# Conditioning vector on the GpSimd queue, attention output by channel instead of by token with crossbar transposes

## Chip, core and metric

The kernel runs on one core of a Trainium2 chip. The metric is the device time of one execution in microseconds, the median of several runs. The engines named below are TensorE (PE, with its weight loads as PEld), VectorE (DVE), ScalarE (ACT), GpSimd (POOL) and SyncE (SP). SP here only issues DMAs and waits.

## What is computed

The attention half of a diffusion transformer block with adaptive layer norm. B = 2 batches, N = 256 tokens, D = 1152 channels, all arrays bf16:

```
mod = (silu(c) @ w_mod).reshape(B, 6, 1, D)
shift_a, scale_a, gate_a = mod[:, 0], mod[:, 1], mod[:, 2]      # the other three are not used
h = layernorm(x) * (1 + scale_a) + shift_a
q, k, v = split(h @ wqkv)
p = softmax(q @ k.T * D ** -0.5)
out = x + gate_a * (p @ v @ wo)
```

## The kernel before

The 512 tokens are four tiles of 128 (tiles 0 and 1 are batch 0, tiles 2 and 3 batch 1), and the 1152 channels are nine blocks of 128. Every operation goes through `op` (line 35), which records the engine, what is read and what is written. `emit` (line 72) turns this into one stream per engine with semaphore waits. So each engine, and each queue of DMAs, runs in the order in which the operations are recorded. A DMA queue is the instruction stream of the engine that issues it: the loads of x tile 2, 0 and 1 and all weights stand in SP's, those of `c` (line 295) and of x tile 3 (line 297) in ACT's. POOL begins with the identity matrices and small constants (lines 322 to 329).

**Start.** `ORDER` (line 169) writes out by hand how the engines' first work is interleaved. PE turns `c` (`cT`, line 506), then x tile 2, runs four matmuls on zeros (`warm`), then turns the other x tiles. ACT sums x tile by tile (`sum_x`, line 386) and then makes silu(c) with DVE and POOL, which ends in `scT_sb`: for each block of channels 32 columns, of which the first two are the two batches' values and the others zero. DVE centres and scales the turned x. The scale groups of w_mod (`s_mm`, line 441) and the key weights arrive in pieces, and keys are accumulated block by block into seven banks of PSUM. Queries, values and scores follow.

**From the scores on** (lines 738 to 817). `v_last` computes the last 128 channels of v turned, and a crossbar DMA turns them back. `v_tile(i)` computes the first 1024 channels of v for one token tile, in two pieces of 512. `score` and `softmax` leave the probabilities in `e_sb`, and `p_T` has SP turn them by a crossbar DMA into `pT_sb`. The gate row is `silu(c) @ w_mod[gate]`: 36 matmuls (line 752) put it into a bank in four quarters of 288 channels, each in a strip of 32 partitions. `scr_sb`, a copy of `scT_sb` made by POOL (line 739), repeats each batch's value 16 times, so that each strip has 16 equal rows per batch. Eight DMAs (line 764) copy them to all 128 partitions of `gate_rep`, each of the 16 rows 8 times.

`pv(i)` (line 671) is attention output for one token tile: the stationary operand is `pT_sb` (128 keys by 128 tokens), the moving one `v_sb` in pieces of 384 channels, two matmuls per piece. Three pieces are evacuated by ACT and DVE in turn, and a crossbar DMA on SP turns the tile into `pvT_sb` (channels on partitions), which the output projection reads. `pv(0)` and `pv(1)` come after the first piece of v tile 2, `pv(2)` and `pv(3)` after the projection of tile 0.

**Output projection** (lines 782 to 817). For each token tile, columns in pieces of 384: nine matmuls into one bank (line 792), the gate multiplied by DVE (line 805), x added (line 808), and a store by SP. After each piece of tile 1 DVE multiplies three blocks of `wo` with the gate (`fold`, line 773); tile 3's last columns use these and have the residual added in one step (line 797). Banks are taken in a ring of eight (`next_bank`, line 647).

Of the kernel before, what the change touches and what calls it, by code (L numbers as in the profile page):

```python
# [6 lines left out]
ALU = mybir.AluOpType  # L7
# [3 lines left out]
PE = mybir.EngineType.PE  # L11
DVE = mybir.EngineType.DVE
AC = mybir.EngineType.Activation
POOL = mybir.EngineType.Pool
SP = mybir.EngineType.SP
# [6 lines left out]
class _Prog:  # L22
# [12 lines left out]
    def op(self, eng, fn, r=(), w=(), dma=False, extra=()):  # L35
        o = _Op()
        o.eng, o.fn, o.dma = eng, fn, dma
        o.sem = o.val = None
        o.inc = False
        deps = set(extra)  # L40
        for k in r:
            if k[0] == "ps":
                continue
            p = self.last_w.get(k)
            if p is not None and not (p.eng == eng == PE):
                deps.add(p)
            self.readers.setdefault(k, []).append(o)
        for k in w:
            if k[0] == "ps":
                continue  # L50
            for q in self.readers.get(k, ()):
                if q is not o and (q.dma or dma or q.eng != eng):
                    deps.add(q)
            p = self.last_w.get(k)
            if p is not None and p is not o and not (p.eng == eng == PE):
                deps.add(p)
            self.readers[k] = [o] if k in r else []
            self.last_w[k] = o
        for k in set(r) | set(w):
            if k[0] != "ps":  # L60
                continue
            accesses = self.bank.setdefault(k, {})
            for e, q in accesses.items():
                if e != eng:
                    deps.add(q)
            accesses[eng] = o
        deps.discard(o)
        o.deps = deps
        self.ops.append(o)
        return o  # L70
# [71 lines left out]
B = 2  # L142
NTOK = 256
D = 1152
T = B * NTOK
P = 128
DC = D // P
# [11 lines left out]
GW = 288  # L159
# [37 lines left out]
def _build(nc, es, x, c, wqkv, wo, w_mod, out):  # L197
    bf16 = dt.bfloat16
# [12 lines left out]
    xnT_sb = sb("xnT_sb", [P, DC, T], bf16)  # L211
    hT_sb = sb("hT_sb", [P, DC, T], bf16)
    qkT_sb = sb("qkT_sb", [P, 2 * DC, T], bf16)
    v_sb = sb("v_sb", [P, TT, D], bf16)
# [22 lines left out]
    d1_sb = sb("d1_sb", [P, DC, 2], f32)  # L237
    rc_sb = sb("rc_sb", [P, DC, 2], f32)
    scT_sb = sb("scT_sb", [P, DC, 32], bf16)
    scr_sb = sb("scr_sb", [P, DC, B, 16], bf16)  # L240
    s1_sb = sb("s1_sb", [P, DC, 2], f32)
    sh_sb = sb("sh_sb", [P, DC, 32], f32)
    gaterow_sb = sb("gaterow_sb", [P, GW], bf16)
# [48 lines left out]
        op(SP, lambda e: e.dma_start(wq_sb[:, k0:k1, c0:c1], wq_v[:, k0:k1, c0:c1]),  # L292
           w=[("w", tag, k) for k in range(k0, k1)], dma=True)

    op(AC, lambda e: e.dma_start(c_sb[:, :], c[:, :]), w=[("c",)], dma=True)
    load_x(SP, 2)
    load_x(AC, 3)
    op(AC, lambda a: a.preload_act_table_set("natural_log_exp_and_others"))
# [38 lines left out]
    def evac(eng, dst, src, r, w):  # L337
        if eng == DVE:
            op(DVE, lambda v: v.tensor_copy(dst, src), r=r, w=w)  # L339
        else:  # L340
            op(AC, lambda a: a.activation(dst, src, ACT.Copy), r=r, w=w)  # L341
# [305 lines left out]
    def next_bank():  # L647
        bnk = ring[rot[0] % 8]
        rot[0] += 1
        return bnk  # L650
# [15 lines left out]
        op(SP, lambda e: e.dma_start(v_sb[:, :, c0:c1], vT_sb[:, :], transpose=True),  # L666
           r=[("vT",)], w=[("v", i, 2) for i in range(TT)], dma=True)

    AP_ = [(0, 384), (384, 768), (768, 1152)]

    def pv(i):
        b = i // 2
        for q, (c0, c1) in enumerate(AP_):
            bank = next_bank()
            for sbk in range(2):
                op(PE, lambda pe, sbk=sbk, c0=c0, c1=c1, bank=bank: pe.matmul(  # L676
                    ps[bank][:, 0:c1 - c0], pT_sb[:, b, sbk, (i % 2) * P:(i % 2 + 1) * P],
                    v_sb[:, 2 * b + sbk, c0:c1], start=(sbk == 0), stop=(sbk == 1)),
                   r=[("v", 2 * b + sbk, n) for n in range(3) if VP[n][0] < c1 and VP[n][1] > c0] + [("pT", b, i % 2)],
                   w=[("ps", bank)])  # L680
            evac(AC if (3 * i + q) % 2 == 0 else DVE, bass.AP(xnT_sb, i * D + c0, [[DC * T, P], [1, c1 - c0]]),
                 ps[bank][:, 0:c1 - c0],
                 [("ps", bank)], [("at", i, q)])
        op(SP, lambda e: e.dma_start(pvT_sb[:, :, i * P:(i + 1) * P], bass.AP(xnT_sb, i * D, [[DC * T, P], [1, D]]), transpose=True),
           r=[("at", i, q) for q in range(3)], w=[("pv", i)] + [("h0", cc, i) for cc in range(DC)], dma=True)

    def v_tile(i, pieces=(0, 1)):
        for q in pieces:
            c0, c1 = VP[q]
            bank = next_bank()  # L690
            for k in range(DC):
                op(PE, lambda pe, k=k, c0=c0, c1=c1, bank=bank: pe.matmul(  # L692
                    ps[bank][:, 0:c1 - c0], hT_sb[:, k, i * P:(i + 1) * P], wq_sb[:, k, 2 * D + c0:2 * D + c1],
                    start=(k == 0), stop=(k == DC - 1)),
                   r=[("w", "v", k), ("hT", k, i // 2)], w=[("ps", bank)])
            nev[0] += 1
            dst, src, sc = v_sb[:, i, c0:c1], ps[bank][:, 0:c1 - c0], rstd_sb[:, i:i + 1]
            rk, wk = [("ps", bank), ("rstd", i)], [("v", i, q)]
            if nev[0] % 2:
                op(AC, lambda a, dst=dst, src=src: a.activation(dst, src, ACT.Copy, scale=sc), r=rk, w=wk)  # L700
            else:
                op(DVE, lambda v, dst=dst, src=src: v.tensor_scalar(dst, src, sc, None, op0=ALU.mult), r=rk, w=wk)  # L702
# [30 lines left out]
    def p_T(i):  # L733
# [1 line left out]
        op(SP, lambda e: e.dma_start(pT_sb[:, b, :, qt * P:(qt + 1) * P], e_sb[:, i, :], transpose=True),  # L735
           r=[("e", i)], w=[("pT", b, qt)], dma=True)

    src = bass.AP(scT_sb, 0, [[DC * 32, P], [32, DC], [1, B], [0, 16]])
    op(POOL, lambda g: g.tensor_scalar(scr_sb[:, :, :, :], src, 1.0, 0.0, op0=ALU.mult, op1=ALU.add),
       r=[("scT",)], w=[("scr",)])  # L740
    v_last()
    v_tile(0)
    sbanks = [score(i) for i in range(TT)]
# [6 lines left out]
    for k in range(DC):  # L750
        for j in range(4):
            op(PE, lambda pe, k=k, j=j, bank=bank: pe.matmul(  # L752
                ps[bank][32 * j:32 * (j + 1), 0:GW], scr_sb[:, k, :, :],
                wgate_ap[:, k, j * GW:(j + 1) * GW], start=(k == 0), stop=(k == DC - 1)),
               r=[("wgate",), ("scr",)], w=[("ps", bank)])
    op(AC, lambda a, bank=bank: a.activation(gaterow_sb[:, :], ps[bank][:, 0:GW], ACT.Copy),
       r=[("ps", bank)], w=[("grow",)])
    v_tile(2, (0,))
    pv(0)
    pv(1)  # L760
    for b in range(B):
        for j in range(4):
            row = bass.AP(gaterow_sb, (32 * j + 16 * b) * GW, [[GW, 16], [0, 8], [1, GW]])
            op(SP, lambda e, b=b, j=j, row=row: e.dma_start(gate_rep[:, b, j * GW:(j + 1) * GW], row),
               r=[("grow",)], w=[("gate", b, j)], dma=True)
    v_tile(2, (1,))
    v_tile(3)


    LC = 768  # L770
# [11 lines left out]
    for i in range(TT):  # L782
        b = i // 2
        cols = [(0, 384), (384, 768), (768, 1152)] if i < TT - 1 else [
            (0, 384), (384, 768), (768, 1024), (1024, 1152)]
        for (c0, c1) in cols:
            n = c1 - c0
            bank = next_bank()
            gated = i == TT - 1 and c0 >= LC
            for k in range(DC):  # L790
                rhs = wog_ap[:, k, c0 - LC:c1 - LC] if gated else wo_ap[:, k, c0:c1]
                op(PE, lambda pe, i=i, k=k, rhs=rhs, n=n, bank=bank: pe.matmul(  # L792
                    ps[bank][:, 0:n], pvT_sb[:, k, i * P:(i + 1) * P], rhs,
                    start=(k == 0), stop=(k == DC - 1)),
                   r=[("pv", i), ("wog", k) if gated else ("wo",)], w=[("ps", bank)])
            if gated:
                op(DVE, lambda v, i=i, c0=c0, c1=c1, n=n, bank=bank: v.tensor_tensor(  # L797
                    xo_sb[:, i, c0:c1], ps[bank][:, 0:n], x_sb[:, i, c0:c1], ALU.add),
                   r=[("ps", bank), ("x", i)], w=[("o", i, c0)])
                store(i, c0, c1)  # L800
                continue
            s = nst[0] % 4
            nst[0] += 1
            gk = [("gate", b, j) for j in range(4) if j * GW < c1 and (j + 1) * GW > c0]
            op(DVE, lambda v, b=b, c0=c0, c1=c1, n=n, bank=bank, s=s: v.tensor_tensor(  # L805
                ga_sb[:, s, 0:n], ps[bank][:, 0:n], gate_rep[:, b, c0:c1], ALU.mult),
               r=[("ps", bank)] + gk, w=[("ga", s)])
            op(DVE, lambda v, i=i, c0=c0, c1=c1, n=n, s=s: v.tensor_tensor(
                xo_sb[:, i, c0:c1], x_sb[:, i, c0:c1], ga_sb[:, s, 0:n], ALU.add),
               r=[("x", i), ("ga", s)], w=[("o", i, c0)])  # L810
            store(i, c0, c1)
            if i == 0 and c1 == D:
                pv(2)
                pv(3)
            if i == 1:
                for k in range(nst[0] % 3 * 3, nst[0] % 3 * 3 + 3):
                    fold(k)
# [34 lines left out]
```

## Time and profile before

| What | Value |
|---|---|
| median of 3 runs | 98.04 us (97.77 to 98.43) |
| profiled execution | 97.77 us, of it 96.0 us from the first to the last instruction |
| granted TensorE clock | 1.000 (mean) |
| chain that ended last | PE 75%, SP's queue 10%, DMA 9% of the span |
| matmuls of L676 (attention output) | 24, 128x384 |
| crossbar transposes of `pvT_sb` | 4, 3.3 us from issue to landing |
| gate row DMAs (L764) | 8 of 72 KB, 2.7 us from issue to landing |
| transposes of `pT_sb` | 4, 2.3 us to landing |

The span counts from the first instruction of the program to the last; the time of the execution lies around it. A row of the chain of waits reads: start in us, length in us, engine, what it writes, line, how many. A row of the timeline adds the operation, its output and input, and in brackets how long the engine had been idle and what ended that. "ACTq" and "SPq" are DMA issues in the queue of ACT and SP; how long a DMA then takes to land stands apart.

### The profile page before, as it was taken

The page shows a single profiled execution, that of the slowest core. Times are in us where ns is not written, and L with a number is a line of the kernel's source. Part 1 is how long each engine was busy: PE and PEld are TensorE (multiplying, and loading weights), DVE is VectorE, ACT ScalarE, POOL GpSimd, SP SyncE. Part 2 cuts the span into 40 slices and gives each one's busy share as a digit, 9 for nine tenths or more (in the row PEclk, how much of TensorE's full clock was granted, in tenths as well). Part 3 has the DMA queues.
Part 4 walks back from the last instruction along what each step waited for, and adds up shares of the span by engine and source line. Part 5 has one row for each costly group of instructions (what it writes and reads, how often), then busy time and mean ns, then how long its engine had stood idle before and what let it go on. Part 6 is the DMA issues. An engine that isn't in the chain of part 4 may idle for free.

```text
span 96.0 us, 1715 instructions
## 1 busy us (share of the span) xinstructions
PE 90.6 (94%) x685; PEld 49.8 (52%) x693; DVE 51.6 (54%) x133; ACT 31.7 (33%) x65; POOL 2.4 (2%) x13
## 2 busy tenths in 40 slices
PE   5998899979999999999999999999999999999990
PEld 1666555444544454444444487455544655665570
DVE  1157984840458649305602075564631567899571
ACT  2778897956541200004120203336402014000000
POOL 5040000000000000000000000000000000000000
PEclk9999999999999999999999999999999999999999
DMA  2999999999999999999999993111296742931222
GB/s 50 332 294 355 328 314 350 352 321 336 363 366 366 381 339 353 387 394 390 393 391 393 391 330 75 38 27 27 46 200 106 123 98 76 206 94 43 91 70 82
DMA packets 25403, 23.21 MB, mean 242 GB/s; under 512 B 7346, under 2 KB 21426, under 8 KB 25396
## 3 DMA queue, kind: packets, MB, share of 16 engines
q1 hardware_dynamic: 25248, 22.81, 78.4%
q10 hardware_dynamic: 148, 0.30, 1.0%
q8 instruction: 5, 0.08, 0.3%
q14 instruction: 2, 0.02, 0.1%
HBM read 19.76 MB, written 1.18 MB: 218 GB/s over the span
## 4 chain that ended last, share of the span: by engine, by line
PE 75%; SPq 10%; DMA 9%; issue 1%; ACT 1%; DVE 0%
PE psbank L492 28%; PE psbank L792 18%; PE psbank L692 16%; DMA wm_sb<-in_w_mod_dram 9%; SPq L292 7%; PE psbank L708 4%; PE psbank L676 4%; PE psbank L660 2%; SPq L285 1%; PE psbank L436 1%; SPq L281 1%; PE psbank L752 1%; ACT qkT_sb L341 1%; PE psbank L415 0%; DVE xo_sb L797 0%
## 5 line engine op out<-in xcount | busy, mean ns | idle before, releaser
L492 PE MATMUL psbank<-pvT_sb,wq_sb 128*128 128x512 bf16 (+1 forms) x82 | 18.0, 366 | 0.7 <-DVE pvT_sb L477 0.3
L492 PE MATMUL psbank<-hT_sb,wq_sb 128*128 128x512 bf16 x79 | 17.5, 379 | 0.2 <-issue 0.2
L792 PE MATMUL psbank<-wm_sb,pvT_sb 128*128 128x384 bf16 x99 | 16.4, 326 | 0.0
L692 PE MATMUL psbank<-wq_sb,hT_sb 128*128 128x512 bf16 x70 | 15.8, 379 | 0.2 <-issue 0.2
L792 PEld LDWEIGHTS psbank<-wm_sb,pvT_sb 128*128 128x128 bf16 x99 | 9.7, 98 | 6.5
L492 PEld LDWEIGHTS psbank<-hT_sb,wq_sb 128*128 128x128 bf16 x81 | 7.9, 98 | 9.4
L492 PEld LDWEIGHTS psbank<-pvT_sb,wq_sb 128*128 128x128 bf16 x86 | 7.9, 98 | 8.3 <-DVE pvT_sb L477 0.6
L341 ACT ACTIVATE qkT_sb<-psbank 128x512 bf16<-128x512 f32 x9 | 5.0, 603 | 19.5 <-PE psbank L492 19.5
L692 PEld LDWEIGHTS psbank<-wq_sb,hT_sb 128*128 128x128 bf16 x72 | 7.0, 98 | 8.2 <-DVE nb_sb L723 0.2
L339 DVE CAST qkT_sb<-psbank 128x512 bf16<-128x512 f32 x9 | 5.7, 684 | 9.2 <-PE psbank L492 9.2
L805 DVE TENSOR_TENSOR ga_sb<-psbank,gate_rep 128x384 bf16<-128x384 f32 x11 | 6.1, 555 | 4.2 <-PE psbank L792 4.2
L485 DVE SCALAR_TENSOR_TENSOR hT_sb<-std_sb,sh_sb,pvT_sb 128x256 bf16<-128x256 f32 x18 | 7.3, 480 | 0.1
L702 DVE TENSOR_SCALAR v_sb<-psbank,rstd_sb 128x512 bf16<-128x512 f32 x4 | 3.0, 750 | 7.7 <-PE psbank L692 7.7
L341 ACT ACTIVATE xnT_sb<-psbank 128x384 bf16<-128x384 f32 (+2 forms) x9 | 4.7, 546 | 6.5 <-PE psbank L676 6.4
L383 DVE TENSOR_TENSOR xnT_sb<-xnT_sb,nm_sb 128x512 bf16<-128x512 bf16 (+1 forms) x9 | 5.6, 656 | 0.0
L700 ACT ACTIVATE v_sb<-psbank,rstd_sb 128x512 bf16<-128x512 f32 x4 | 2.7, 682 | 7.9 <-PE psbank L692 7.9
L399 ACT ACTIVATE junk_sb<-x_sb,nmu_sb 128x1152 bf16<-128x1152 bf16 x4 | 5.0, 1251 | 0.1
L333 PE MATMUL psbank<-warm_sb 128*128 128x512 bf16 x9 | 3.9, 590 | 1.2 <-DVE warm_sb L320 1.2
L388 ACT ACTIVATE junk_sb<-x_sb 128x1152 bf16<-128x1152 bf16 x4 | 4.6, 1159 | 1.0 <-DMA x_sb<-in_x_dram 1.0
L725 ACT ACTIVATE e_sb<-s_sb,nb_sb 128x256 bf16<-128x256 bf16 x4 | 2.0, 508 | 8.2 <-DVE nb_sb L723 8.2
L339 DVE COPY xnT_sb<-psbank 128x512 bf16<-128x512 bf16 (+1 forms) x5 | 2.1, 447 | 4.1 <-PE psbank L349 4.0
L676 PE MATMUL psbank<-v_sb,pT_sb 128*128 128x384 bf16 x24 | 4.2, 326 | 0.0
(73 smaller groups left out, 73.1 us busy)
## 6 DMA issues: line engine op xcount, KB each, us to landing
wq_sb<-in_wqkv_dram SPq DMA_DIRECT2D x3, 864.0 KB, 11.0
wm_sb<-in_w_mod_dram SPq DMA_DIRECT2D x1, 2592.0 KB, 16.1
wm_sb<-in_wo_dram SPq DMA_DIRECT2D x1, 2592.0 KB, 21.8
wq_sb<-in_wqkv_dram SPq DMA_DIRECT2D x4, 448.0 KB, 8.3
wm_sb<-in_w_mod_dram SPq DMA_DIRECT2D x3, 576.0 KB, 7.5
wm_sb<-in_w_mod_dram SPq DMA_DIRECT2D x1, 1440.0 KB, 11.0
wq_sb<-in_wqkv_dram SPq DMA_DIRECT2D x6, 224.0 KB, 6.9
wq_sb<-in_wqkv_dram SPq DMA_DIRECT2D x2, 576.0 KB, 10.1
```

The source lines that it names most:

```text
L292: op(SP, lambda e: e.dma_start(wq_sb[:, k0:k1, c0:c1], wq_v[:, k0:k1, c0:c1]), w=[("w", tag, k) for k in range(k0, k1)], dma=True)
L339: op(DVE, lambda v: v.tensor_copy(dst, src), r=r, w=w)
L341: op(AC, lambda a: a.activation(dst, src, ACT.Copy), r=r, w=w)
L383: op(eng, lambda e: e.tensor_tensor(ap, ap, nm, ALU.add), r=[("xnT", cc, i) for i in tiles] + nk, w=[("xnT", cc, i) for i in tiles])
L388: op(AC, lambda a: a.activation(junk_sb[:, :], x_sb[:, i, :], ACT.Copy, scale=sc, accum_out=dst[:, i:i + 1]), r=[("x", i)], w=[("junk", 0) ...
L399: op(AC, lambda a: a.activation(junk_sb[:, :], x_sb[:, i, :], ACT.Square, bias=nmu_sb[:, i:i + 1], scale=1.0, accum_out=sq_sb[:, i:i + 1]) ...
L485: op(DVE, lambda v: v.scalar_tensor_tensor(hT_sb[:, cc, lo:hi], std_sb[:, lo:hi], sh_sb[:, cc, b:b + 1], h0T_sb[:, cc, lo:hi], op0=ALU.mul ...
L492: op(PE, lambda pe: pe.matmul(ps[bank][:, lo:hi], wq_sb[:, k, col * P:(col + 1) * P], src[:, k, lo:hi], start=(k == 0) if start is None el ...
L676: op(PE, lambda pe, sbk=sbk, c0=c0, c1=c1, bank=bank: pe.matmul(ps[bank][:, 0:c1 - c0], pT_sb[:, b, sbk, (i % 2) * P:(i % 2 + 1) * P], v_s ...
L692: op(PE, lambda pe, k=k, c0=c0, c1=c1, bank=bank: pe.matmul(ps[bank][:, 0:c1 - c0], hT_sb[:, k, i * P:(i + 1) * P], wq_sb[:, k, 2 * D + c0 ...
L792: op(PE, lambda pe, i=i, k=k, rhs=rhs, n=n, bank=bank: pe.matmul(ps[bank][:, 0:n], pvT_sb[:, k, i * P:(i + 1) * P], rhs, start=(k == 0), s ...
L805: op(DVE, lambda v, b=b, c0=c0, c1=c1, n=n, bank=bank, s=s: v.tensor_tensor(ga_sb[:, s, 0:n], ps[bank][:, 0:n], gate_rep[:, b, c0:c1], ALU ...
```

## The change

The conditioning vector's DMA moves from ACT's queue to POOL's, where it stands ahead of the identity and constants. x tile 3 is then the first DMA on ACT's queue.

`pv` becomes a function of a batch and a pair of channel blocks. The stationary operand is now `v_sb` (128 keys by 128 channels), the moving one `pT_sb` of a whole batch (256 tokens), and the result is already turned: two channel blocks share a bank and go by one evacuation straight into `pvT_sb`. There are five pairs per batch, the last with one block. The four crossbar transposes go. All ten calls stand after v tile 3 and before the projection, instead of in two places.

`scr_sb` and its copy go: the gate matmuls read `scT_sb` itself, so each strip has one row per batch, and each gate DMA reads that row 128 times. These DMAs no longer have transposes of `pvT_sb` before them on SP.

```
-    scr_sb = sb("scr_sb", [P, DC, B, 16], bf16)
...
-    op(AC, lambda e: e.dma_start(c_sb[:, :], c[:, :]), w=[("c",)], dma=True)
+    op(POOL, lambda e: e.dma_start(c_sb[:, :], c[:, :]), w=[("c",)], dma=True)
     load_x(SP, 2)
     load_x(AC, 3)
...
-    AP_ = [(0, 384), (384, 768), (768, 1152)]
-    def pv(i):
...
-                    ps[bank][:, 0:c1 - c0], pT_sb[:, b, sbk, (i % 2) * P:(i % 2 + 1) * P],
-                    v_sb[:, 2 * b + sbk, c0:c1], start=(sbk == 0), stop=(sbk == 1)),
...
-        op(SP, lambda e: e.dma_start(pvT_sb[:, :, i * P:(i + 1) * P], bass.AP(xnT_sb, i * D, [[DC * T, P], [1, D]]), transpose=True),
-           r=[("at", i, q) for q in range(3)], w=[("pv", i)] + [("h0", cc, i) for cc in range(DC)], dma=True)
...
-    src = bass.AP(scT_sb, 0, [[DC * 32, P], [32, DC], [1, B], [0, 16]])
-    op(POOL, lambda g: g.tensor_scalar(scr_sb[:, :, :, :], src, 1.0, 0.0, op0=ALU.mult, op1=ALU.add),
-       r=[("scT",)], w=[("scr",)])
...
-                ps[bank][32 * j:32 * (j + 1), 0:GW], scr_sb[:, k, :, :],
+                ps[bank][32 * j:32 * (j + 1), 0:GW], scT_sb[:, k, :],
...
-    v_tile(2, (0,))
-    pv(0)
-    pv(1)
     for b in range(B):
         for j in range(4):
-            row = bass.AP(gaterow_sb, (32 * j + 16 * b) * GW, [[GW, 16], [0, 8], [1, GW]])
+            row = bass.AP(gaterow_sb, (32 * j + b) * GW, [[GW, 1], [0, P], [1, GW]])
...
-    v_tile(2, (1,))
+    v_tile(2)
     v_tile(3)
+    def pv(b, pair):
+        ccs = [cc for cc in (2 * pair, 2 * pair + 1) if cc < DC]
+        bank = next_bank()
+        for h, cc in enumerate(ccs):
+            for sbk in range(2):
+                op(PE, lambda pe, h=h, cc=cc, sbk=sbk: pe.matmul(
+                    ps[bank][:, h * NTOK:(h + 1) * NTOK],
+                    v_sb[:, 2 * b + sbk, cc * P:(cc + 1) * P], pT_sb[:, b, sbk, :],
+                    start=(sbk == 0), stop=(sbk == 1)),
+                   r=[("v", 2 * b + sbk, cc // 4), ("pT", b, 0), ("pT", b, 1)], w=[("ps", bank)])
+        n = len(ccs)
+        evac(AC if pair % 2 == 0 else DVE,
+             pvT_sb[:, ccs[0]:ccs[0] + n, b * NTOK:(b + 1) * NTOK],
+             ps[bank][:, 0:n * NTOK].rearrange("p (c t) -> p c t", c=n),
+             [("ps", bank)], [("pv", cc, b) for cc in ccs] + [("h0", cc, 2 * b + n) for cc in ccs for n in (0, 1)])
+    for b in range(B):
+        for pair in range(5):
+            pv(b, pair)
...
-                   r=[("pv", i), ("wog", k) if gated else ("wo",)], w=[("ps", bank)])
+                   r=[("pv", k, b), ("wog", k) if gated else ("wo",)], w=[("ps", bank)])
...
-            if i == 0 and c1 == D:
-                pv(2)
-                pv(3)
```

More of the change, by code (lines that the diff above doesn't have):

```diff
@@ L667, in v_last, with v_tile @@
            r=[("vT",)], w=[("v", i, 2) for i in range(TT)], dma=True)
-    AP_ = [(0, 384), (384, 768), (768, 1152)]
-    def pv(i):
[L672 to L676, printed above, removed]
-                    ps[bank][:, 0:c1 - c0], pT_sb[:, b, sbk, (i % 2) * P:(i % 2 + 1) * P],
-                    v_sb[:, 2 * b + sbk, c0:c1], start=(sbk == 0), stop=(sbk == 1)),
[L679 to L683, printed above, removed]
-        op(SP, lambda e: e.dma_start(pvT_sb[:, :, i * P:(i + 1) * P], bass.AP(xnT_sb, i * D, [[DC * T, P], [1, D]]), transpose=True),
-           r=[("at", i, q) for q in range(3)], w=[("pv", i)] + [("h0", cc, i) for cc in range(DC)], dma=True)
-    def v_tile(i, pieces=(0, 1)):
-        for q in pieces:
-            c0, c1 = VP[q]
+    def v_tile(i):
+        for q, (c0, c1) in enumerate(VP[:2]):
             bank = next_bank()
@@ L752, in _build @@
             op(PE, lambda pe, k=k, j=j, bank=bank: pe.matmul(
-                ps[bank][32 * j:32 * (j + 1), 0:GW], scr_sb[:, k, :, :],
+                ps[bank][32 * j:32 * (j + 1), 0:GW], scT_sb[:, k, :],
                 wgate_ap[:, k, j * GW:(j + 1) * GW], start=(k == 0), stop=(k == DC - 1)),
-               r=[("wgate",), ("scr",)], w=[("ps", bank)])
+               r=[("wgate",), ("scT",)], w=[("ps", bank)])
     op(AC, lambda a, bank=bank: a.activation(gaterow_sb[:, :], ps[bank][:, 0:GW], ACT.Copy),
        r=[("ps", bank)], w=[("grow",)])
-    v_tile(2, (0,))
-    pv(0)
-    pv(1)
     for b in range(B):
         for j in range(4):
-            row = bass.AP(gaterow_sb, (32 * j + 16 * b) * GW, [[GW, 16], [0, 8], [1, GW]])
+            row = bass.AP(gaterow_sb, (32 * j + b) * GW, [[GW, 1], [0, P], [1, GW]])
             op(SP, lambda e, b=b, j=j, row=row: e.dma_start(gate_rep[:, b, j * GW:(j + 1) * GW], row),
                r=[("grow",)], w=[("gate", b, j)], dma=True)
-    v_tile(2, (1,))
+    v_tile(2)
     v_tile(3)
+    def pv(b, pair):
[16 more added lines that the diff above has]
+            pv(b, pair)
     LC = 768
```

## The prediction

> **What bounds the kernel now.** I read the share table, then the chain of waits in order of time, then the two ends of the timeline.
>
> ```profile
> PE 90.6 (94%) x685; PEld 49.8 (52%) x693; DVE 51.6 (54%) x133; ACT 31.7 (33%) x65; POOL 2.4 (2%) x13
> ```
>
> ```profile
> 11.01 8.80 DMA wm_sb<-in_w_mod_dram
> 19.81 0.04 issue
> 19.86 0.57 PE psbank L436 x36
> ...
> 63.05 1.22 PE psbank L752 x36
> 64.27 0.16 issue
> 64.42 1.89 PE psbank L692 x8
> 66.31 1.95 PE psbank L676 x12
> 68.27 5.83 PE psbank L692 x27
> 74.09 4.39 PE psbank L792 x27
> 78.48 1.95 PE psbank L676 x12
> 80.43 13.20 PE psbank L792 x90
> 93.63 0.02 issue
> 93.65 0.29 DVE xo_sb L797
> ```
>
> Up to 19.81 us the chain is loads: the last scale group of w_mod lands then, and PE waits for it. From 19.86 to 93.63 it is PE almost without a break, and from 64.42 each piece begins where the one before ends. So attention output (L676) costs its PE time and nothing else; the crossbar transposes after it are hidden. An edit there pays only in PE time or by making PE wait. An edit at the start pays only if it moves PE at 19.86. The timeline of the start:
>
> ```profile
> 0.74 0.55 ACTq L295 DMA_DIRECT2D c_sb<-in_c_dram  x1
> ...
> 1.32 0.37 ACTq L281 DMA_DIRECT2D x_sb<-in_x_dram  x1
> ...
> 3.44 0.40 PE L507 MATMUL psbank<-ident,c_sb 2*128 2x2 bf16 x9
> ...
> 3.56 1.16 ACT L388 ACTIVATE junk_sb<-x_sb 128x1152 bf16<-128x1152 bf16 x1 [0.55 <-DMA x_sb<-in_x_dram]
> ...
> 4.70 1.59 PE L333 MATMUL psbank<-warm_sb 128*128 128x512 bf16 x4
> ```
>
> PE turns c before x tile 2, in program order. The x transfers take 2.8, 4.4, 4.4 and 4.6 us to land (group of x_sb; the two middle ones by its median): tile 2 at 3.54, tiles 0 and 3 at 5.5 to 5.7, tile 1 at 6.3. The semaphore writes of c in the trace end at 2.44.
>
> [...] 162.5 ns for 384 columns, 109 for 256. The trace agrees: 12 in 1.95 us (162.5), and the 36 score matmuls of 256 columns with a weight load each in 3.93 us (109). [...] here ScalarE's first packet runs 0.92 us after the issue, and no GpSimd DMA is in the trace. [...] the trace has both queues (q1, q10) but not yet contending from the first byte. [...] no transfer of before reads a single partition.
>
> **The change, part by part.**
>
> *Attention output.* Removed: 24 matmuls of 384 columns, 24 × 0.1625 = 3.90 us. Added: 9 × 2 × 2 = 36 of 256, 36 × 0.109 = 3.93. On the path: **+0.03**. The weight loads are 98 ns each, below 109, as in the scores.
>
> Evacuation, removed: 6 ACT copies of 0.49 and 6 DVE casts of about 0.58 (1.86 and 1.64 per three). Added: 4 ACT copies of 512 columns (0.60), 2 of 256 (about 0.4), 4 DVE casts of 0.68. One bank takes PE 0.44 us; ACT and DVE alternate, each with 0.87 us a bank, so neither falls behind. What could wait: the first projection tile needs batch 0's banks, and batch 1's 18 matmuls (1.96 us) lie between. Batch 1 needs v tile 3, whose DVE evacuation (0.75) is covered by batch 0's 1.96 us of PE. pT is issued by 66.33 and lands at most 2.9 us later, before PE reaches it at 64.42 + 7.72 = 72.1. Cost 0; without the cover, under 1 us once.
>
> *Queues.* SP loses four transposes (1.3 us of issue, 3.3 to landing each), all hidden now: gain 0. What is late next is PE itself, which is already the bound. The gate rows' eight issues (0.6 each) no longer stand behind two of these and start after the last pT, at 66.3 rather than 70.6. GpSimd's copy into scr (0.43, at 6.41) goes; nobody waits for it.
>
> *Gate rows.* The 36 matmuls keep their shape (32 weight columns, 288 wide): 1.22 us as now. But each row is now read 128 times from one partition, not from 16: 128 × 576 B = 74 KB. Before it lands in 2.7 us. [...] The first gate multiply comes at 72.1 + 3.93 + 1.46 = 77.5, the first fold at about 82.8. Bounds: nothing if as quick as now; late if four times slower. I take hidden.
>
> *Start.* c leaves ScalarE's queue: x tile 3 issues at 0.74, not 1.32. On GpSimd, the DMA stands before ident, ident32, eps and the scT memset (0.21, 0.29, 0.30, 0.10, 0.34). [...] Waiting behind c on PE are tile 2's transposes, four warm matmuls (1.59) and all later transposes. c has 3.51 − 2.44 = 1.0 us of cover from the first warm matmuls. Lower bound: c as now; upper: 2 us later, 4.4. I take 0.5 to 1 later: no wait of its own.
>
> The other side: [...] By 3.5 us some 500 KB had moved; giving ScalarE's queue up to 288 KB more ahead of tile 2's end, at the 320 GB/s of those slices, delays tile 2 by up to 0.8 us. I take 0.4 (x at 3.9 to 4.0). PE then slips about 0.2 to 0.4, up to the first key block at 10.18. From there to 19.86 PE has idle time in which to make it up: windows 10.18 to 12.20, 15.40 to 16.30 and 16.30 to 19.86 show 0.05 + 0.08 + 0.39 = 0.52 us. [...] Cost: 0 to 0.3 beyond cover, I take **+0.05**. Tile 3's earlier landing earns nothing, since PE would only reach the same load wait sooner.
>
> *Tail.* Eleven gate multiplies and adds (0.56 + 0.36), nine folds (0.35) and the last store are unchanged; DVE loses six casts. PE still ends it: 0.
>
> Sum, against the profiled execution's 97.77 (span 96.0 and 1.8 around it): +0.03 + 0.05 = 97.85. That execution is 0.27 below the median of 98.04, so 98.1 as a median.
>
> **Rivals.** A run of this kernel can tell about 1% (1.0 us) from no change.
>
> *No change* (0.57): as summed, 97.5 to 98.9, likeliest 98.1.
>
> *Slower, the start* (0.22): c through GpSimd, or tile 2 behind tile 3, holds PE more than the 0.52 us of idle covers. Place: c's turn at 3.44. It decides from c landing at about 4.0 (cover to 3.51, plus 0.52); each microsecond after costs one, with up to another microsecond if PE's pause puts off its full clock into the key block (it is granted at 5.83 us now, and the warm matmuls' records shrink there from 634 to 380 ns). c at 5.0 gives +1.0 to 2.0: 99.1 to 100.1. For: DVE is 92% busy in the 10 to 15 us window, so little is made up there. Against: 1.0 us of cover on c [...].
>
> *Slower, the gate rows* (0.10): one partition serves all 128 reads and batch 1's gates come after about 84.3 (fold at 82.8 plus the 1.5 us by which DVE idles later). [...] For: single-partition reads are not in the trace. [...]
>
> *Slower otherwise* (0.03): a PE wait on the evacuations, 99 to 100.
>
> *Faster* (0.08): GpSimd's queue costs nothing, tile 3's earlier landing takes out the PE waits before 20 us, and the load at 19.81 comes earlier too as the queue fills sooner. PE idle before 20 us is 0.37 + 0.23 + 0.46 from 5 us on, about 1.1: 97.0. Against: that load's place on SP is unchanged. The change not doing what it says (tile 3 lands no earlier, as the engines are full from 2.5 us on) ends in no change.
>
> **Numbers.** Faster 0.08, same 0.57, slower 0.22 + 0.10 + 0.03 = 0.35. The range 97.4 to 99.8 leaves out the gate case (0.10), the upper end of the start cases (0.06) and half of the faster one (0.04). The no-change case alone is 97.5 to 98.9.
>
> **What the profile would show.** Right: one unbroken run of PE from about 64.4, with 36 matmuls of 256 in 3.9 us before the projection and none waiting; the c transposes at about 3.5 and x tile 2's at about 4; the load wait at 19.8 still there or just gone; gate rows landed by 80. Wrong: PE idle at c's transposes past 4.5 us, the chain running through GpSimd or c instead of SP's loads before 20 us; DVE's gate multiplies or folds waiting for a DMA; or a projection starting later than 3.9 us after the last v tile.

## The result, and the profile after

The changed kernel takes 100.89 us in the median of 6 runs (100.20 to 101.20), against 98.24 for the kernel before beside it (97.77 to 98.53): a ratio of 1.0259, 95% interval 1.0211 to 1.0306. It is slower by about 2.6 us, where no change was the likeliest case, and lies above the range of 97.4 to 99.8. The profiled execution took 100.28 us with a span of 98.5, so 1.8 us lie around the span as before: the whole loss is inside it.

The share table and then the chain of waits of the changed kernel, in order of time (start, length, what):

```profile
PE 91.3 (93%) x697; PEld 51.7 (53%) x705; DVE 51.1 (52%) x131; ACT 32.2 (33%) x65; POOL 2.7 (3%) x13
```

```profile
1.25 4.37 DMA c_sb<-in_c_dram
5.62 0.14 issue
5.75 0.37 PE psbank L506 x9
6.13 1.07 PE psbank L348 x9
7.20 1.71 PE psbank L332 x4
...
22.43 0.50 PE psbank L435 x36
...
65.56 1.22 PE psbank L729 x36
66.77 0.16 issue
66.93 7.72 PE psbank L672 x35
74.65 3.93 PE psbank L750 x36
78.58 17.59 PE psbank L788 x117
96.17 0.02 issue
96.19 0.29 DVE xo_sb L793
```

Line numbers are up to 26 lower than before, where code went. The chain's beginning is new: not SP's queue and the scale group's load, but the DMA of c, which takes 4.37 us to land, and then PE's own work without a load in between. The scale group's matmuls (L435 here, L436 before) start at 22.36, not 19.86: **2.50 us**. (The chain has 22.43, as it begins a piece where the one before it ends.) The timeline has them so:

```profile
22.36 0.57 PE L435 MATMUL psbank<-wm_sb,scT_sb 128*32 128x96 bf16 x36
```

From the gate rows' matmuls on, everything is the kernel before, later by that: PE's run to the last projection piece lasts 66.93 to 96.17, 29.24 us, where it lasted 64.42 to 93.63, 29.21. So 2.50 of the 2.54 by which PE ends later are there before 23 us.

The start in the timeline, changed kernel:

```profile
0.74 0.39 ACTq L280 DMA_DIRECT2D x_sb<-in_x_dram  x1
...
1.25 0.73 POOL L294 DMA_DIRECT2D c_sb<-in_c_dram  x1 [0.80 <-POOLq L830]
...
4.82 1.16 ACT L387 ACTIVATE junk_sb<-x_sb 128x1152 bf16<-128x1152 bf16 x1 [2.39 <-DMA x_sb<-in_x_dram]
...
5.75 0.37 PE L506 MATMUL psbank<-ident,c_sb 2*128 2x2 bf16 x9 [2.25 <-DMA c_sb<-in_c_dram]
```

x tile 3 does issue at 0.74, as the change says. c's issue on GpSimd starts at 1.25 and takes 0.73. PE has done its five zero matmuls at 3.5 and stands for 2.25 us; x tile 2 (4.8) would be there, but its transposes are queued behind c. After c, PE is also slower. In the groups of x_sb, the durations (minimum, median, maximum in ns) of the 36 transposes are, before and then after:

```profile
L349 PE MATMUL psbank<-ident,x_sb x36: 216/219/314, 3.8 to 9.7; 128*128 128x128 bf16 x36
```

```profile
L348 PE MATMUL psbank<-ident,x_sb x36: 216/314/314, 6.1 to 12.6; 128*128 128x128 bf16 x36
```

The median has gone from the quick value to the slow one. (It is a coarse sign: in e1_only_c below, with nearly the same start, it is still 219.) The trace's clock record begins its stretch of full TensorE clock at 5.83 us before and at 10.26 after. The first matmuls on the keys, which need x and c turned, come 2.96 us later, before and then after:

```profile
10.18 2.13 PE L492 MATMUL psbank<-pvT_sb,wq_sb 128*128 128x256 bf16 x13 [0.28 <-DVE pvT_sb L477]
```

```profile
13.14 2.13 PE L491 MATMUL psbank<-pvT_sb,wq_sb 128*128 128x256 bf16 x13 [0.28 <-DVE pvT_sb L476]
```

### The profile page after: what moved, and what is told of

Read it like the earlier page. It is cut to its first block, busy times and chain, and to the rows that moved or that the text cites. A ratio compares the mean times of both kernels' runs of the same rounds, so it can differ in the third digit from the quotient of the medians.

```text
span 98.5 us, 1730 instructions
## 1 busy us (share of the span) xinstructions
PE 91.3 (93%) x697; PEld 51.7 (53%) x705; DVE 51.1 (52%) x131; ACT 32.2 (33%) x65; POOL 2.7 (3%) x13
## 3 DMA queue, kind: packets, MB, share of 16 engines
HBM read 19.76 MB, written 1.18 MB: 213 GB/s over the span
## 4 chain that ended last, share of the span: by engine, by line
PE 88%; DMA 4%; DVE 2%; issue 2%; ACT 1%; POOLq 0%
PE psbank L491 34%; PE psbank L788 18%; PE psbank L672 16%; DMA c_sb<-in_c_dram 4%; PE psbank L750 4%; PE psbank L688 4%; PE psbank L348 3%; PE psbank L659 2%; PE psbank L332 2%; PE psbank L435 1%; PE psbank L729 1%; DVE xnT_sb L382 1%; PE psbank L426 1%; PE psbank L363 1%; ACT qkT_sb L340 1%
## 5 line engine op out<-in xcount | busy, mean ns | idle before, releaser
L804 DVE TENSOR_TENSOR xo_sb<-x_sb,ga_sb 128x384 bf16<-128x384 bf16 x11 | 3.9, 358 | 0.4
L348 PE MATMUL psbank<-ident,x_sb 128*128 128x128 bf16 x36 | 4.1, 275 | 0.0
```

Of the source, the lines that this page charges most:

```text
L348: op(PE, lambda pe, cc=cc, bank=bank, lo=lo: pe.transpose(psb[bank][:, lo:lo + P], x_sb[:, i, cc * P:(cc + 1) * P], ident[:, :]), r=[("x", ...
```

## The experiments

Each run is timed against the kernel before on the same chip, whose median was 97.9 in these. A table first, as the runs answer one another. "Key block" is the start of the first key matmuls of 256 columns, "group 3" that of the scale group's matmuls near 20 us; times in us, from each kernel's profiled execution; the landing of c and the full clock are from the trace's semaphore and clock records. The ratio comes from several executions, the other columns from one: the full clock in particular scatters. Four profiles whose PE starts alike (before, e2_rest, e7_gate_one, e8_gate_16) have it at 5.83, 7.24, 6.22 and 6.93.

| Run | c landed | full clock | key block | group 3 | ratio to before (95% interval) |
|---|---|---|---|---|---|
| before | 2.44 | 5.83 | 10.18 | 19.86 | 1 |
| changed | 5.62 | 10.26 | 13.14 | 22.36 | 1.0259 (1.0211 to 1.0306) |
| e1_only_c | 5.70 | 9.75 | 13.07 | 22.29 | 1.0228 (1.0172 to 1.0284) |
| e2_rest | 2.95 | 7.24 | 10.63 | 19.85 | 1.0001 (0.9967 to 1.0034) |
| e3_c_behind | 4.62 | 8.24 | 11.85 | 21.07 | 1.0132 (1.0078 to 1.0185) |
| e4_x_first | 5.70 | 8.40 | 12.12 | 21.34 | 1.0171 (1.0110 to 1.0233) |
| e5_warm | 5.64 | 4.25 | 11.33 | 20.55 | 1.0056 (1.0028 to 1.0084) |
| e9_c_twice2 | 5.53 | 10.76 | 13.33 | 22.55 | 1.0254 (1.0201 to 1.0308) |
| e10_both | 5.39 | 5.44 | 11.11 | 20.80 | 1.0060 (1.0038 to 1.0083) |
| e11_no_warm | 2.13 | 9.65 | 11.54 | 20.76 | 1.0040 (1.0018 to 1.0062) |

### c alone, and all but c

e1_only_c, on the kernel before:

```
-    op(AC, lambda e: e.dma_start(c_sb[:, :], c[:, :]), w=[("c",)], dma=True)
+    op(POOL, lambda e: e.dma_start(c_sb[:, :], c[:, :]), w=[("c",)], dma=True)
```

> The kernel before with c alone moved to the GpSimd queue. Theory 1 (c's late landing is the whole loss): PE waits some 2.2 us for c at its turn, the full clock comes late, about 0.4 us is absorbed at the load wait near 20 us; +2.5 us, ratio 1.024 to 1.030, c landing about 5.6 us. Theory 2 (part of the loss is in the attention output or the gate rows): less than +2.0 us here, the rest in the kernel with the other parts.

e2_rest is the changed kernel with that line turned back.

> The changed kernel with c back on ScalarE's queue, ahead of x tile 3: attention output by channel and one-partition gate rows remain. Theory 1: no change against the kernel before, ratio 0.998 to 1.003 (+0.03 us of matmuls). Theory 2: slower by 0.5 us or more, with PE idle or DVE waiting for gate rows after 64 us.

100.25 us for the first (ratio just under the 1.024 expected, its interval overlapping that of the whole change), 97.93 for the second, beside 97.93 for the kernel before. The one moved line is the loss, as far as these intervals tell; attention output by channel, without transposes, and one-partition gate rows come to nothing measurable together (within 0.4%). Theory 1 stands.

### Is it GpSimd, or x tile 3 going first?

e3_c_behind has c on ScalarE's queue again, but behind x tile 3:

```
-    op(POOL, lambda e: e.dma_start(c_sb[:, :], c[:, :]), w=[("c",)], dma=True)
     load_x(SP, 2)
     load_x(AC, 3)
+    op(AC, lambda e: e.dma_start(c_sb[:, :], c[:, :]), w=[("c",)], dma=True)
```

> The changed kernel with c on ScalarE's queue but behind x tile 3. It has x tile 3's early issue and none of GpSimd. Theory A (tile 3's packets hold tile 2 up, and c among them): tile 2 lands at 4.5 to 4.8 us, PE turns it about 1 us later than before, +0.7 to +1.5 us. Theory B (only GpSimd's descriptor path is slow): c lands before 3.5 us and tile 2 before 3.9, within 0.3 us of the kernel before.

99.23 us, +1.3. The timeline of e3_c_behind:

```profile
1.18 0.54 ACTq L296 DMA_DIRECT2D c_sb<-in_c_dram  x1
...
4.76 0.38 PE L506 MATMUL psbank<-ident,c_sb 2*128 2x2 bf16 x9 [1.26 <-DMA c_sb<-in_c_dram]
```

Issued 0.44 us later than before, c lands 2.2 us later (4.62 against 2.44). No GpSimd is in this. Tile 3, ahead of c on the same queue, lands at 4.47; tile 2 lands at 4.28 rather than 3.54, a little sooner than theory A had it. The time falls in theory A's range and theory B is out, although c was again the later of the two. From almost the same issue time (1.18 and 1.25), GpSimd then adds another 1.0 us (5.62 against 4.62). Part of that may be how its DMA ends: c's landing has 16 semaphore updates in the changed kernel, from 4.77 to 5.62, against three with ScalarE here, the last two at 4.59 and 4.62. No run separates this.

e6_c_alone makes all x loads wait for c, so that GpSimd's DMA has the engines to itself:

```
     def load_x(eng, i):
-        op(eng, lambda e: e.dma_start(x_sb[:, i, :], x_pi[:, i, :]), w=[("x", i)], dma=True)
+        op(eng, lambda e: e.dma_start(x_sb[:, i, :], x_pi[:, i, :]), r=[("c",)], w=[("x", i)], dma=True)
```

> The changed kernel with all four x tiles' loads made to wait for c, and so the weights queued behind them on SyncE: c goes through GpSimd with no other load running. Only c's issue and landing are of interest. Theory D (the other loads' packets hold c up): it lands 2.0 to 2.5 us after its issue instead of 4.4. Theory E (GpSimd's own path is that slow): 3.8 us or more. The kernel's time is worse by 2 to 5 us, as the loads start later.

The landing in c_sb's group of e6_c_alone, minimum, median and maximum of one DMA:

```profile
DMA to landing us min/median/max: 1.9/1.9/1.9
```

1.9 us from GpSimd when alone, 4.4 beside the x tiles: theory D. In the trace's packets, the first of GpSimd's queue runs at 2.54 alone and at 4.26 in the changed kernel, 0.57 and 2.29 us after GpSimd has finished the issue at 1.97. The queue has 32 packets, two of 2304 bytes and 30 of 4, and even those of 4 bytes run from 4.33 on only. ScalarE's c before took 1.7 (0.74 to 2.44), issued beside tile 2's and ahead of all else. The path through GpSimd was not slow by itself (1.9 us); c, 4.6 KB, came late where the x tiles had been issued before it (4.4 us). (The kernel took 101.78 us in its one run, as its loads start 2.5 us later.)

e9_c_twice2 puts tile 3 back to its old issue time by an unused load of c ahead of it:

```
+    c2_load = op(AC, lambda e: e.dma_start(c2_sb[:, :], c[:, :]), w=[("c2",)], dma=True)
     op(POOL, lambda e: e.dma_start(c_sb[:, :], c[:, :]), w=[("c",)], dma=True)
...
-    op(SP, None, extra=outs)
+    op(SP, None, extra=outs + [c2_load])
```

> The changed kernel with a second, unused load of c ahead of x tile 3 on ScalarE's queue, so that tile 3 issues at 1.3 us as before while the c that is used still comes through GpSimd. In the runs so far the scale group's matmuls near 20 us start 9.2 us after the first key block, or at the load's landing (19.8) if that is later, so the end moves by what the first key block passes 10.6 us. Theory F (tile 3's early packets hold c up): c lands by 4.4 us, tile 2 by 3.8, key block at 11.6 or sooner, 98.2 to 99.0. Theory G (tile 2 and tile 0 on SyncE's queue do it just as well, because GpSimd's descriptors come after all of them): c lands at 5.2 us or later although tile 2 lands by 3.8, key block after 12.5, 99.8 or more.

Theory G: tile 2 lands at 3.64 as before, and c still at 5.53; 100.52 us. The early tile 3 delays tile 2 by 1.3 us (4.80 against 3.54), but that isn't the loss. The chain of e9_c_twice2 begins as the changed kernel's does:

```profile
1.24 4.29 DMA c_sb<-in_c_dram
5.53 0.14 issue
5.67 0.37 PE psbank L508 x9
```

### What PE's stand costs

In all runs in which group 3's load was not the later one, group 3 starts 9.22 us after the key block (13.14 and 22.36, 11.85 and 21.07, 11.33 and 20.55). Before, the key block at 10.18 would allow 19.40, and the load makes it 19.86: 0.46 us of cover.

e4_x_first moves c's transposes behind those of tile 2 on PE:

```
-    ('sum', 2), ('cT',), ('cTo',), ('xT', 2, 0), ('e1',), ('xT', 2, 1), ('warm', 4), ('sum', 0), ('xT', 3, 1),
+    ('sum', 2), ('xT', 2, 0), ('xT', 2, 1), ('cT',), ('cTo',), ('e1',), ('warm', 4), ('sum', 0), ('xT', 3, 1),
```

> The changed kernel with PE turning x tile 2 before c. Theory 1 (what c costs is PE standing still with other work behind it): x tile 2 is turned from 4.9 us, beside the wait for c, and about 0.9 us of the loss of 2.5 comes back: 99.9 to 100.1. If the silu chain behind c (scT, the first scale group) sets the end instead, nothing comes back: 100.7 to 101.

The key block comes 1.02 us sooner, and the ratio falls by 0.009, some 0.9 us, though c lands as late as ever. What queues behind c on PE had cost that, the clock's share included: PE goes on at 5.01 instead of 5.75, and the full clock comes at 8.40.

e5_warm fills the stand with zero matmuls (`WARM = 5` becomes `WARM = 10`):

> The changed kernel with ten zero matmuls at the start in place of five, which fill PE's wait for c from 3.5 to 5.6 us. Theory C (0.65 us of the loss is the full clock coming at 10.3 us instead of 5.8, because PE paused): clock granted before 8 us, first key block at 12.5 or sooner instead of 13.1, 0.4 to 0.7 us faster than the changed kernel (100.2 to 100.5). Rival (the pause costs only itself): the clock's time or the end does not move, 100.8 to 101.

98.42 us: some 2.0 us of the loss are gone (ratio 1.0259 to 1.0056), three times what theory C had. c is no earlier, and PE still turns it at 5.78. The timeline of e5_warm:

```profile
1.19 3.82 PE L332 MATMUL psbank<-warm_sb 128*128 128x512 bf16 x10 [1.19 <-DVE warm_sb L319]
...
5.78 0.36 PE L506 MATMUL psbank<-ident,c_sb 2*128 2x2 bf16 x9 [0.77 <-DMA c_sb<-in_c_dram]
6.07 0.68 PE L348 MATMUL psbank<-ident,x_sb 128*128 128x128 bf16 x9
6.58 1.03 PE L332 MATMUL psbank<-warm_sb 128*128 128x512 bf16 x4
```

Nine transposes in 0.68 us, four zero matmuls in 1.03; in the changed kernel 1.14 and 1.91. From c's turn to the key block it takes 5.55 us with the full clock from the start, 6.74 before, 7.39 in the changed kernel. The 0.65 that I had put down to the clock was the difference to a kernel that is itself at the slow clock for part of that stretch. It also rests on one profile each: from c's turn to the key block the four profiles named above have 6.75 to 7.20 us, and the three with c late and five zero matmuls (changed, e1_only_c, e9_c_twice2) 7.23 to 7.66; the means are 0.46 apart.

e11_no_warm is the control: the kernel before without its five first zero matmuls (`WARM = 0`), so that the clock moves while c and x land as before.

> The kernel before without its five zero matmuls at the start; c and x land as before. It moves the clock alone. Theory C (a later full clock delays the key block by itself): clock granted at 7 to 8.5 us, first key block at 10.7 to 11.3, of which only what passes 10.6 reaches the end: +0.1 to +0.7 us. Rival (the clock in this stretch is worth nothing): key block at 10.2 to 10.4, no change.

Full clock at 9.65, later than expected; key block 1.36 us later with c and x where they were, group 3 0.90 later, and 0.4 us on the median time (the profiled execution, at 98.65, is one of the longer ones). Theory C's direction holds, with 0.46 us of it covered.

e10_both takes e4's order and e5's ten matmuls together:

> The changed kernel with ten zero matmuls at the start and PE turning x tile 2 before c. If the loss is PE's pause plus the late clock and nothing else, both are covered: clock granted before 6 us, first key block at 10.6 or sooner, the load near 19.8 sets the end again, 97.8 to 98.3, as fast as the kernel before with c still landing at 5.6 us. If c's silu chain has a cost of its own, 98.7 or more.

98.66 us (97.73 to 99.08), not the time of the kernel before: a miss. The clock came at 5.44, but the ten matmuls occupy PE to 5.6 although tile 2 is there at 4.4, so the key block is at 11.11. That allows 20.33; in this profile the scale group's load landed only at 20.75, on the chain:

```profile
11.56 9.19 DMA wm_sb<-in_w_mod_dram
20.75 0.04 issue
20.80 0.57 PE psbank L435 x36
```

The load landed anywhere from 19.7 to 21.3 us over these profiles. Why it scatters wasn't tried. The silu chain behind c, the rival here, is not what held the key block: its result `scT_sb` was ready at 7.80, and PE first read it at 9.93.

### The gate rows

e7_gate_one is the kernel before with one-partition rows:

```
-            row = bass.AP(gaterow_sb, (32 * j + 16 * b) * GW, [[GW, 16], [0, 8], [1, GW]])
+            row = bass.AP(gaterow_sb, (32 * j + b) * GW, [[GW, 1], [0, P], [1, GW]])
```

with the matmuls reading `scT_sb`.

> The kernel before with the gate rows read from one partition each instead of 16, all else as before. In the changed kernel the eight rows took from 68.9 to about 86.5 us to land, 17.6 us in all. Here they are issued from 70.6 on, so by the same length they land at about 88, while the first fold comes at 82.8: DVE stops for some 5 us, of which 1.5 is made up: +2 to +4 us. If the length depends on the queue before them and not on the partition, or the tail has more slack than I read, no change.

106.42 us, ratio 1.0862 (1.0783 to 1.0941): +8.5, twice what was expected. Waits of e7_gate_one (in total, times, longest, us):

```profile
DVE ga_sb L805 <- DMA gate_rep<-gaterow_sb: 5.1, 2, 3.1
PE psbank L792 <- DMA pvT_sb<-xnT_sb: 5.0, 1, 5.0
DVE wq_sb L774 <- DMA gate_rep<-gaterow_sb: 3.5, 1, 3.5
```

I had counted DVE's stops alone. SP's eight issues take 13.1 us (70.5 to 83.6) rather than 5.2, so the stores (from 83.7) and the second pair of transposes (from 87.6) stand behind them; PE waits 5.0 us for these, and its clock is halved from 88.1 to 95.0 (the window from 88 to 95 shows 0.51 granted, those around it 1.00).

e8_gate_16 is the changed kernel with c on ScalarE and 16-partition rows:

> The changed kernel with c back on ScalarE's queue and the gate rows read from 16 partitions again: attention output by channel is the only part of the change left. The gate rows land within 8 us of their first issue and DVE never waits for them. Theory 1 (PE sets the end, both forms hidden): same time as the kernel before, ratio 0.997 to 1.003. Rival (the tail in the changed kernel had become DVE's): 0.3 us or more faster than with one-partition rows.

98.04 us, ratio 1.0002 (0.9974 to 1.0030), rows landed 7.2 us after the first issue (66.3 to 73.5). With one-partition rows (e2_rest) they take from 66.4 to 84.0 and DVE's first fold waits 1.2 us, and the time is the same: hidden. Against e7_gate_one, the rows are issued 4 us sooner and no transpose that PE waits for stands behind them. No version beat the kernel before.

## Why the prediction was wrong

The sum was +0.08 us, and about +2.6 was measured. Step by step:

- **Attention output, +0.03: right.** 36 matmuls in 3.93 us, PE's run 0.03 longer, no wait on an evacuation; e8_gate_16 has it alone, the same time within 0.3%.
- **Queues, 0: right.** The transposes were hidden, and taking them off SP earned nothing by itself. With one-partition rows it kept PE from waiting, as e7_gate_one has the transposes and PE waits 5.0 us for them.
- **Gate rows, hidden: right, with a wrong size.** They were to have landed by 80, which was my estimate; nothing in the profile of before showed a row read from one partition. They came at 86.57 (84.0 in e2_rest, whose time scale is that of before): 2.2 us per row (17.6 over eight). In the changed kernel's packets from 70 to 84 mostly 22 to 32 reads of 576 bytes begin in each half microsecond, so 25 to 37 GB/s for all rows together, with a few bursts of up to 93 reads; with 16 partitions (the kernel before, from 72 to 77) 64 to 154 reads. The end is near the 84.3 from which I had let them decide. DVE waited 1.2 us and made it up, as the 1.5 us of slack said.
- **Start, c's landing: the step that failed.** "I take 0.5 to 1 later: no wait of its own", with an upper bound of 2 us. c landed 3.2 us later, at 5.62, and PE stood 2.25 us for it. I had priced the path alone, by an estimate, and it was indeed short: 0.73 of issue, 1.9 us to landing when alone (e6_c_alone). What I left out is what stands in front. With the x tiles issued ahead, the queue's first packet ran only at 4.26, against 2.54 with nothing ahead. e3_c_behind shows a late landing from ScalarE too (4.62), but there c stood behind tile 3 in one queue; in the changed kernel it has a queue of its own. That two packets of 2.3 KB would be served at once from a queue of their own was my assumption, and the trace does not show it: 2.29 us passed between the end of the issue and the first packet. What delays them stays open.
- **Start, tile 2 behind tile 3: too small.** 1.26 us, not 0.4 or at most 0.8; it did not set the time, as c was later (e9_c_twice2).
- **Cover of 0.52 us before 19.86: right**, 0.46 by the key block's distance.
- **The clock.** It stood in the rival alone ("up to another microsecond"). Between these two profiles it cost 0.65, with the scatter named above.

At group 3 the sum is 2.31 (c's turn on PE, 3.44 to 5.75) + 0.65 (6.74 to 7.39 us from there to the key block) − 0.46 (cover) = 2.50. That divides the 2.50 between these two profiles and is no second proof of it; in e5_warm c's turn is as late, and at the full clock most of the loss is gone. The rival "Slower, the start" had mechanism and price: from 4.0 one for one makes 1.6 at 5.62, with up to 1 for the clock 2.6. It failed only in its chance, because c's landing was bounded too low; even the bound taken, 4.4, lay past the 4.0 from which the rival let c cost.

## What to carry to other kernels

The cost of this small load was its place among the large ones far more than its own path (4.4 us to landing against 1.9): ask which transfers are already issued when it is issued, and give a load that a whole engine's order hangs on the first place in an early queue. Before moving a wait, list what is queued in order behind the instruction that waits; here other work that was ready stood behind 4.6 KB. Where TensorE stands still at the start, count the slow clock afterwards too: the full clock came at 10.26 us with the stand and at 4.25 with zero matmuls in it, and filling it brought back some 2.0 of the 2.5 us.

## What was not expected of the hardware

c, 4.6 KB, issued 0.44 us later on the same queue but behind one x tile, landed 2.2 us later. Ten zero matmuls without a gap had the full clock at 4.25 us in one profile and 5.44 in another; five, followed by transposes, at 5.8 to 7.2; none at 9.65; five and a pause before the next work at 8.2 to 10.8 (11.95 in e6_c_alone, where x comes later still). Rows of 74 KB each read from one partition took 2.2 us apiece on average, and their issue on SP grew from 0.60 to 1.7 us in the median.
